# Packed attention with a gated convolution: a subtraction moved to VectorE, one product in plain float32 on small tiles, more store buffers at the end, and a new issue order

## The chip, the cores and the metric

The kernel runs on one core of a Trainium2 chip. The metric is the device time of one execution in microseconds. Five engines work side by side, each through its own queue in order: TensorE (PE in the profile, with PEld for its weight loads), VectorE (DVE), ScalarE (ACT), GpSimd (POOL) and SyncE (SP), whose queue issues all DMAs of this kernel.

## The reference

There are 8 batches, 8 heads, 576 positions and a head size of 64; `p` holds 32 packed queries for each head. Every head attends twice, and the result goes through a gated convolution:

```python
p_packed = sm_attn(p, k, v)                # 32 x 64 for each batch and head
out = sm_attn(q, p_packed, p_packed)       # 576 x 64 for each batch and head
x = out.transpose(0, 2, 1, 3).reshape(B, S, H * D)
gate_pre = sum(conv_w[k] * xp[:, k:k + S, :] for k in range(5))   # xp: 4 rows of zeros ahead of x
gate = 1.0 / (1.0 + np.exp(-gate_pre))
val = x @ w_val
result = (gate * val) @ w_out              # 8 x 576 x 512
```

`sm_attn` is a softmax over scaled scores with 1e-9 added to the sum, and a product with the values. The weights of the gated part come as 64-bit floats and are turned into pairs of 32-bit words on the chip.

## The kernel before, in words

Positions and channels are laid so that 128 partitions are always in use. The eight heads of a batch form two groups g of four heads; a group's 32 packed queries of four heads fill 128 partitions. The 576 positions are two halves of 288.

Each batch goes through these steps; the letter is the stream's name in the order table.

- K, V, Q, P load a batch's inputs (SP), L the weights. C, W and O turn the convolution weights, `w_val` and `w_out` into float32 words (ACT, DVE and POOL in turn).
- k and q: PE turns blocks of k and q (tiles kpt and qpt), ACT copies them to SBUF (kT, qT). k also turns p (pTt, pT).
- a: scores `s<-kT,pT` on PE, their maximum nb on DVE, the exponential a1 on ACT, its turn on PE (at) with a copy (a1t), then the product pv on PE. ACT writes it, divided by the sum, twice side by side into ppd; DVE writes it again times a mask of ones and zeros into pp, so that each head has zeros beside it.
- p: PE turns ppd (ppTt), ACT copies it (ppT).
- s: scores `s<-qT,ppT` for each group; DVE transposes 32x32 blocks (t2), takes the maximum mx; POOL subtracts it, ACT takes the exponential.
- t: DVE sums (sm) and inverts (rs), POOL multiplies, DVE transposes back (a2). ACT rounds a2 to the type float32r (a2h), and DVE writes the rest (a2l).
- w: wp = ppT times the value weights on PE, and again a rounded part wph (ACT) and a rest wpl (DVE).
- x: the attention's output for the convolution. pp too is split (pph on ACT, ppl on POOL), and PE makes three products for each pair of heads: pph with a2h, ppl with a2h, pph with a2l. ACT copies the result into xp behind its zeros, which POOL writes.
- g: the gate, sig: one product on ACT, four multiply-adds on DVE (`sig<-xp,cw,sig`), a tanh on ACT, for each of four blocks n4 of 128 channels.
- v: val = 12 float32r products on PE for each block; DVE multiplies with the gate (`sig<-sig,val`), ACT rounds it (gvh), and POOL writes the rest (gvl). The last of all 32 blocks is on DVE.
- o: the output product, 12 float32r products of gvh, gvl with woh, wol for each of nine chunks of 128 rows of a pair of batches (four in the even batch's turn, five in the odd one's); ACT copies it to osb, and SP stores it. In the last batch the five chunks 4 to 8 are summed block by block in PSUM while the last blocks of val are made; chunks 5 and 7 are copied by DVE.

Tiles named by a tag take turns in a small number of buffers (`NB`). A tile's next use waits until the last reader of its buffer is done. PSUM gives two "big" tiles, shared by s, x, wp and val, three "mid" tiles and one "out" tile. osb has two buffers, a2 one, t2 two.

The order of the work is a table (`ORDER`): each token takes one step (or, with .n, n steps) of one stream for one batch, for example `g3.2`. A step issues one or a few instructions, and each engine runs its own in the order in which the table issues them. Nothing is moved later; a wait on one engine holds everything behind it in that engine's queue. Line 94 of the profile is the helper that issues every instruction, so that groups go by tile names.

Of the kernel before, what the change touches and what calls it, by code (L numbers as in the profile page):

```python
# [48 lines left out]
ORDER = """
K0 L0.3 V0 P0 W0.13 L0 W0 L0 W0 L0 Q0 W0 K0 W0 k0 P1 W0 k0.4 W0 k0.2 W0 C0 W0 k0 C0 a0 W0 C0 W0 a0 W0 a0 q0 C0  # L50
O0 C0 q0.2 C0 O0 q0.2 C0 O0 q0 k0 O0 C0 k0.2 O0 L0 k0.2 V0 O0.2 K1 L0 k0 K1 O0 a0 Q0 O0 L0 k1 P2 a0 k1 O0 a0.3
O0 a0.4 O0 a0.2 O0.2 a0.2 O0 a0.6 O0.2 a0.2 O0 k1 a0.2 O0 p0 x0 k1.2 p0 x0 k1.2 s0 k1 O0.2 w0 s0 O0 x0 s0 a1 w0
O0 k1 s0 a1 k1.2 w0 a1 s0 q0 O0 k1.2 t0 q0.2 k1 q0.2 a1 O0 q0 t0 s0 V1 a1 V1 O0.3 Q1 t0 a1 Q1 a1.2 K2 O0 a1.2 s0
P3 a1.2 k2 t0 s0 k2 O0 a1 O0.2 s0 a1 t0 x0 s0 O0 a1.4 x0.2 t0 a1.2 x0.2 O0 a1.4 g0 t0 a1 p1 a1 q1 p1 g0 q1.2 w1
q1 t0 q1 g0 t0 w1 O0 g0 q1.2 w1 O0 q1.2 s1 O0 k2 q1 O0 s1 q1 K2 k2.2 V2 O0 s1 q1 Q2 k2.2 V2 k2 Q2 s1 K3 a2 P4 O0
s1.2 a2 s1 a2 k2 g0 k2.2 s1 g0 t0 v0 k2 g0 s1 t1 k2 s1 x0 v0 t1 k2 k3 | v0 a2 g0 x0 q2 k3 a2 v0 x0 q2 t1 q2 a2.3
x0 g0 v0 a2 q2 g0 x1 t1 x1 a2 q2 a2 t1 a2 q2.2 g0 a2.2 q2 t1 g0 x1 q2 g0 x1 v0 t1 a2 k3 q2 a2 x1 K3 x1 a2 V3 k3
g0 k3 Q3 v0 q2 P5 t1 k3.2 v0 q2 a2 t1 v0 k3 g0 a2 x1 t1 a2.3 g0 k3 a2.2 k3 g0 k3 a2.2 g0 p2 a3 g0 v0 p2 g0 k3.2
s2 v0 a3 k3 k4 v0 s2 a3 q3 s2 a3 q3 V3 g0 Q3 v0 K4 k4 a3 s2 K4 P6 a3.2 g0 a3 q3 s2 w2 g0 a3 q3 t2 g0 x1 a3 q3
a3.2 w2 v0 t2 a3.2 w2 v0 s2 q3 v0 g1 t2 o0 a3.2 t2 a3 g1 t2 s2 v1 o0 g1 s2 a3 g1 q3 a3.2 s2 x1 q3 o0 a3 Q4 o0 V4  # L60
x1 g1 s2 g1 t2 g1 v1 a3 t2 o0 k4 a3.2 o0 v1 g1 x1 k4 V4 t2 a3 v1 p3 x1 v1 a3 p3 t2 g1 x2 s3 t2 g1 q3 k4 s3 x2
q3.2 k4 o0 g1 q3 Q4 s3 g1 x2 g1 s3 v1.2 g1 q4 s3 k4 v1 q4.2 o0 K5 s3 k4 o0 q4 g1 k4 a4 s3 k4.2 g1 v1 k4 s3 g1 o0
a4 s3 g1.2 v1 a4 g1 s3 g1 v1 x2 o0 q4 g1 x2.2 o0 v1 q4 Q5 q4 x2 v1 q4 g1.2 x2.2 t3 g2 k4 v1 t3 x2 q4 K5 k4 k5 x2
v1 P7 g2 a4 q4 t3 x2 v1 o1 k5 a4 t3 x3 g2 a4.2 x3 t3 a4 o1 k5 t3 a4.2 o1 v2 k5 a4 g2 t3 a4 o1 a4 g2 t3 g2.2 v2
t3 q4 g2 v2 k5 Q5 t3 a4 q4 k5 g2 k5 o1 V5 w3 a4.2 v2 o1 k5 a4 K6 a4 k5 g2 a4.2 w3 o1 g2 k5 w3 a4 x3 g2.3 v2 o1
g2 o1 g2 o1 v2 g2 v2 g2 v2 g2 v2 o1 g2 o1 k5 g2 a4 x3 k5 v2 a4.2 g2 x3.2 v2 g2 V5 k5 a4 x3 a4 p4 v2 a5 K6 k5 p4
v2 g2 a5 x3 g3 a5 g3 o1 v2 g3 v2 g3 a5 v2 o1 v3 o1 a5 g3 a5 o2 a5 g3.2 v3 g3 v3 g3 a5 o2 k6 s4 v3 a5 o2 k6 x3 s4
q5 x3 a5 g3 x3 q5 a5 v3 s4 x3 g3 x4 s4 g3 a5 q5 g3 v3 o2 x4 s4 x4 g3 a5 q5 v3 t4 v3 a5 o2 s4 o2 a5.2 t4 V6 a5.2
q5 s4 a5.2 v3 q5 Q6 g3 a5 t4 g3 q5 t4 a5 s4 k6 q5 a5 w4 g3 k6 t4 g3 q5 k6 s4 g3 v3 a5 k6 w4 g3 x4 V6 o2 v3 g3 s4
w4 v3 x4 a5 q5 a5 t4 p5 o2 k6 g3 p5 q5 o2 k6.2 q5 t4 x4 Q6 k6 K7 s5 x4 g3 k6 s5 v3 g3 x4 t4 g4 k6 s5 t4 a6 g4 k6  # L70
v3 s5 q6 k6 K7 o2 a6 q6 v3 g4 s5 t4 a6 g4 t5 a6 o2 s5 o2 v3 a6 o3 s5 a6 t5 a6 s5 g4 t5 s5 g4 v4 g4 s5 g4 a6 o3
q6 v4 a6.2 o3 t5 x4 g4 a6.2 v4 o3 t5 a6 g4 q6 x4 t5 v4 a6 o3 x4 o3 t5 a6.2 V7 a6 v4 x4 g4 x5 t5 x5 g4 q6 a6 g4
x5 v4 x5 Q7 a6.2 q6 g4 w5 x5 g4 a6 v4 x5 g4 t5 q6 x5 a6 t5 o3 a6 g4 q6 w5 v4 g4 w5 g4 a6 o3 g4 q6 o3 a6.2 k7 g4
p6 q6 V7 v4 k7 g4 p6 g4 q6 v4 g4 x5 k7 Q7 x5 g5 s6 k7 g5 x5 k7 v4 g5 x5 k7 o3 s6 v4 q6 x5 s6 x6 g5 x6 v4 s6 o3.2
g5 s6 k7 v4 w6 g5 k7 t6 v4 s6 g5 o3 v4 s6 w6 s6 t6 w6 s6 k7 t6 o3 v5 k7 g5 o3 s6 g5 t6 o4 v5 g5 v5 t6 g5 k7 o4
t6 x6.2 g5 o4 a7 v5 k7 x6 k7 a7 g5 o4 t6 k7 a7 g5 t6 g5 x6 t6 a7 o4 t6 x6 o4.2 g5 a7 g5 a7.2 g5.2 a7 q7 a7.2 g5
o4 v5 a7 o4 g5 q7 g5 a7 q7 a7 v5 a7 q7 g5 v5 o4 a7.2 v5 g5 a7 g6 x6 g6.2 a7 o4 x6 a7 g6 a7 o4 v5 x6 g6 a7 g6 a7
v5 q7 g6 x6 a7 g6 v5 a7 q7 g6 q7 x6 v5.2 a7.2 q7 x7.2 p7 v5 q7 p7 q7.2 g6 s7 v5 g6 w7 q7 s7 v5 g6 o5 g6 s7 w7 x7
g6 s7 w7 v6 o5 g6 s7 o5 g6 s7 v6 o5 g6 v6 s7 g6 v6 t7 g6 v6 g6 o5 s7 t7 o5.2 v6 s7 t7 v6 g6 s7 t7 v6.2 o5.2 g6
o5 t7.2 v6 t7 v6 x7 g6 o5 x7.2 t7 v6 o5.2 g6 t7 x7.2 t7 g7 x7 g7 o5 v6 g7 o5 x7 g7 x7 v6 x7 g7 v6 g7 v6 o6 g7.2  # L80
v7 o6 g7 o6 g7 o6 v7 g7 v7 g7 v7 g7 v7 o6 g7 o6 g7 o6 v7 g7 v7 g7 v7.2 o6 g7 o6 g7 o6 v7 g7 v7 g7 v7.2 o6.2 g7
o7 g7.2 v7.2 o7 v7 o7.17
"""


# [574 lines left out]
```

## Time and profile before

| | |
|---|---|
| time, median of 3 runs | 331.21 us (329.43 to 331.38) |
| the profiled execution: its own time, its span | 330.79 us, 329.0 us |
| PE busy, weight loads | 287.6 us (87%), 220.6 us |
| DVE busy | 259.0 us (79%) |
| ACT busy | 215.3 us (65%) |
| POOL busy | 123.2 us (37%) |
| DMA | 43.47 MB, 132 GB/s over the span |
| mean granted TensorE clock | 0.976 of full |

The span is the time from the first to the last instruction of the core, and the execution's own time has some 1.8 us around it. A busy PE is not a PE at its peak: matmuls overlap, and a matmul's recorded duration is longer than its place in the queue. Where PE's rate matters, the distance from one group's start to the next group's start is read instead. "x16" behind a row is the number of instructions in it; a plain float32 product of this kernel shows as two records.

### The profile page before, as it was taken

To read this page: it belongs to the slowest core of one execution; us is meant where nothing else is said; L and a number is where in the kernel's file an instruction comes from. 1 tells how busy PE (TensorE), PEld (TensorE's weight loads), DVE (VectorE), ACT (ScalarE), POOL (GpSimd) and SP (SyncE) were. 2 spreads that over 40 slices of the span, in tenths; PEclk is the share of its full clock that TensorE was granted. 3 is DMA by queue.
4 is the path that set the end of the run, shared out by engine and by line. 5 is a ranking of instruction groups with operands and counts; after the bars stand their busy time and mean duration, and the time that the engine had idled before them with its cause. 6 is when DMAs were issued, how large, how long until landed. Compare 5 with 4: busy or idle time off the path is not lost.

```text
span 329.0 us, 7252 instructions
## 1 busy us (share of the span) xinstructions
PE 287.6 (87%) x2932; PEld 220.6 (67%) x2932; DVE 259.0 (79%) x381; ACT 215.3 (65%) x440; POOL 123.2 (37%) x115
## 2 busy tenths in 40 slices
PE   0157987979989999999999898989999999999990
...
DVE  0794288689999999997797999998997899776600
...
PEclk9999997699999999999999999999999999999996
...
GB/s 197 232 255 263 257 162 239 108 230 108 211 217 135 187 166 136 90 241 92 157 34 173 118 237 37 175 87 126 32 66 34 32 35 38 70 53 64 34 24 135
DMA packets 42474, 43.47 MB, mean 132 GB/s; under 512 B 6085, under 2 KB 36805, under 8 KB 42442
## 3 DMA queue, kind: packets, MB, share of 16 engines
...
q8 instruction: 23, 0.38, 0.5%
...
## 4 chain that ended last, share of the span: by engine, by line
PE 40%; DVE 31%; ACT 17%; issue 4%; DMA 3%; POOL 3%; SPq 1%; ACTq 0%; POOLq 0%
DVE sig L94 16%; PE o L94 15%; PE val L94 8%; ACT sig L94 4%; DVE a2l L94 3%; PE x L94 3%; PE s L94 3%; PE kpt L94 3%; PE pv L94 2%; DVE sm L94 2%; PE at L94 2%; DVE t L94 2%; DVE nb L94 2%; DMA wv_words<-in_moe_w_val_dram 2%; PE qpt L94 2%
## 5 line engine op out<-in xcount | busy, mean ns | idle before, releaser
L94 DVE SCALAR_TENSOR_TENSOR sig<-xp,cw,sig 128x576 f32<-128x576 f32 x128 | 122.6, 958 | 11.6 <-ACT sig L94 10.1
L94 POOL TENSOR_TENSOR gvl<-sig,gvh 128x576 fp32r<-128x576 f32 x31 | 49.1, 1584 | 80.0 <-ACT gvh L94 77.0
L94 PE MATMUL o<-woh,gvh 128*128 128x512 f32 x144 | 58.6, 407 | 0.8 <-ACT osb L94 0.8
L94 PE MATMUL o<-woh,gvl 128*128 128x512 f32 x144 | 56.5, 392 | 0.1
L94 PE MATMUL o<-wol,gvh 128*128 128x512 f32 x144 | 56.5, 392 | 0.0
L94 PE MATMUL val<-a2h,wph 128*128 128x288 f32 x128 | 39.6, 309 | 0.5 <-ACT a L94 0.5
L94 PE MATMUL val<-a2l,wph 128*128 128x288 f32 x128 | 37.9, 296 | 0.9 <-DVE a2l L94 0.9
L94 ACT COPY osb<-o 128x512 f32<-128x512 f32 x34 | 19.8, 582 | 28.3 <-PE o L94 22.6
L94 PE MATMUL val<-a2h,wpl 128*128 128x288 f32 x128 | 37.9, 296 | 0.0
L94 PEld LDWEIGHTS o<-woh,gvh 128*128 128x128 f32 x144 | 27.0, 188 | 10.3 <-issue 2.3
L94 ACT CAST gvh<-sig 128x576 fp32r<-128x576 f32 x32 | 21.7, 678 | 17.7 <-DVE sig L94 17.6
L94 POOL TENSOR_TENSOR t<-t,mx 128x576 f32<-128x576 f32 x16 | 24.2, 1513 | 22.0 <-DVE mx L94 22.0
L94 PEld LDWEIGHTS o<-woh,gvl 128*128 128x128 f32 x144 | 27.1, 188 | 6.6 <-POOL gvl L94 0.5
L94 ACT ACTIVATE sig<-sig 128x576 f32<-128x576 f32 x32 | 21.9, 686 | 13.1 <-DVE sig L94 12.9
L94 PEld LDWEIGHTS o<-wol,gvh 128*128 128x128 f32 x144 | 27.1, 188 | 4.6
L94 POOL TENSOR_TENSOR t<-t,rs 128x576 f32<-128x576 f32 x16 | 20.0, 1248 | 23.0 <-DVE rs L94 15.8
L94 DVE SCALAR_TENSOR_TENSOR sig<-sig,val 128x576 f32<-128x576 f32 x32 | 23.7, 741 | 5.6 <-PE val L94 3.0
L94 PE MATMUL qpt<-ident,qm 96*128 96x96 f32 x192 | 26.1, 270 | 1.1 <-ACT kT L94 1.1
L94 PE MATMUL kpt<-ident,km 96*128 96x96 f32 x192 | 26.8, 276 | 0.1
L94 PEld LDWEIGHTS val<-a2h,wph 128*128 128x128 f32 x128 | 24.2, 189 | 3.6 <-ACT a L94 1.2
L94 PEld LDWEIGHTS qpt<-ident,qm 96*128 96x128 f32 x192 | 21.0, 155 | 7.3 <-issue 4.3
L94 PEld LDWEIGHTS kpt<-ident,km 96*128 96x128 f32 x192 | 20.9, 156 | 6.9 <-issue 4.7
...
## 6 DMA issues: line engine op xcount, KB each, us to landing
...
```

Source lines behind the costliest of these rows:

```text
L94: made = getattr(self.engine, op)(*args, **kw)
```

## The change

Five things are changed.

1. gvl, the rest of the gated value, is written by DVE for all 32 blocks.
2. x is made by plain float32 products: for each of four heads one product of ppd (32 partitions, the first of its two copies, 64 columns) with a2 (32 partitions, 288 positions), on tiles of 32 rows and 64 columns of PE's array. Head hl uses rows 32 hl on, columns 64 (hl % 2) on, and writes PSUM bank hl // 2 of the tile. The mask, pp, pph and ppl are gone, ppd has two buffers.
3. So x waits for a2 and ppd alone, and a2's one buffer is held until PE has made x.
4. In the last batch the five chunks 4 to 8 each have a buffer of their own: 4 and 6 keep osb's two, 5 and 7 take t2's two, and 8 takes a2's.
5. The order table is new throughout.

```diff
 NB = {
- 'pp': 2,
- 'ppd': 1,
+ 'ppd': 2,
  'ppT': 2,
- 'pph': 1,
- 'ppl': 1,
...
 ORDER = """
-K0 L0.3 V0 P0 W0.13 L0 W0 L0 W0 L0 Q0 W0 K0 W0 k0 P1 W0 k0.4 W0 k0.2 W0 C0 W0 k0 C0 a0 W0 C0 W0 a0 W0 a0 q0 C0
+x0 L0.5 P0 W0.2 K0 W0 K0 W0 Q0 W0 P1 W0.3 V0 L0 W0 V0 Q0 W0.5 C0 L0 k0 W0 k0 P2 C0 W0 C0 W0 k0 C0 W0 C0 k0.4 K1
...
-    pairs = [slice(2 * NP * pr, 2 * NP * pr + 2 * NP) for pr in range(2)]
-    mask = const.tile([P, 2, D], F32, name="mask")
-    nc.gpsimd.memset(mask, 0.0)
-    for hl in range(4):
-        nc.gpsimd.memset(mask[heads[hl], hl % 2, :], 1.0)
...
-        pp = st["pp", b] = tile_of("pp", [P, G, 2, D], F32, f"pp_{b}")
...
             act.mul(ppd[:, g], pv2, rs)
             yield
-            dve.scalar_tensor_tensor(pp[:, g], pv2, rs, mask, op0=ALU.mult, op1=ALU.mult)
-            yield
...
-        a2 = tile_of("a2", [P, G, S], F32, f"a2_{b}")
+        a2 = st["a2", b] = tile_of("a2", [P, G, S], F32, f"a2_{b}")
...
-        act.copy(pph, pp)
-        yield
-        pool.tensor_tensor(ppl, pp, pph.bitcast(F32), op=ALU.subtract)
-        yield
...
-                ah, al = st["ah", b], st["al", b]
+                pp, a2 = st["ppd", b], st["a2", b]
                 xps = big(f"x_{b}_{g}_{half}")
-                for n, (w, x) in enumerate(((pph, ah), (ppl, ah), (pph, al))):
-                    for pr in range(2):
-                        pe.matmul(
-                            xps[:, pr, :HS],
-                            w[pairs[pr], g, :],
-                            x[pairs[pr], g, hc],
-                            start=(n == 0),
-                            stop=(n == 2),
-                        )
+                for hl in range(4):
+                    pe.matmul(
+                        xps[D * (hl % 2) : D * (hl % 2) + D, hl // 2, :HS],
+                        pp[heads[hl], g, 0, :],
+                        a2[heads[hl], g, hc],
+                        start=True,
+                        stop=True,
+                    )
...
-            (dve if b == B - 1 and n4 == NC - 1 else pool).tensor_tensor(
+            dve.tensor_tensor(
                 lo, gv, hi.bitcast(F32), op=ALU.subtract
             )
...
-            osb = tile_of("osb", [P, DM], F32, f"osb_{b}_{c}")
+            if b == B - 1 and c % 2:
+                osb = tile_of("t2", [P, G, NBLK, NP], F32, f"osb_{b}_{c}")
+                osb = osb.rearrange("a g y z -> a (g y z)")[:, :DM]
+            elif b == B - 1 and c == 8:
+                osb = tile_of("a2", [P, G, S], F32, f"osb_{b}_{c}")[:, 0, :DM]
+            else:
+                osb = tile_of("osb", [P, DM], F32, f"osb_{b}_{c}")
```

On SP's queue the first loads stand in another order. Before (km, vm, qm and p are inputs of batch 0 unless a name comes a second time; wv_words, cw_words and wo_words are the three weights):

```order
L94 DMA km_0_84<-in_k_dram 96x4x384
L94 DMA wv_words<-in_moe_w_val_dram 64x1024 x6
L94 DMA vm_0_95<-in_v_dram 96x4x384
L94 DMA p_97<-in_p_dram 128x2x64 x2
L94 DMA wv_words<-in_moe_w_val_dram 64x1024 x2
L94 DMA cw_words<-in_moe_conv_w_dram 5x1024
L94 DMA wo_words<-in_moe_w_out_dram 128x1024
L94 DMA qm_0_125<-in_q_dram 96x12x128
L94 DMA km_1_128<-in_k_dram 96x4x384
```

And in the changed kernel:

```order
L90 DMA wv_words<-in_moe_w_val_dram 64x1024 x8
L90 DMA cw_words<-in_moe_conv_w_dram 5x1024
L90 DMA p_94<-in_p_dram 128x2x64 x2
L90 DMA km_0_100<-in_k_dram 96x4x384
L90 DMA km_1_103<-in_k_dram 96x4x384
L90 DMA qm_0_106<-in_q_dram 96x12x128
L90 DMA p_109<-in_p_dram 128x2x64 x2
L90 DMA vm_0_116<-in_v_dram 96x4x384
L90 DMA wo_words<-in_moe_w_out_dram 128x1024
```

The value weights now go first as a whole, and batch 0's second k group (km_1) stands ahead of the first block of `w_out` instead of behind it.

On PE, around the first val of batch 0, this stands before in rows 66 to 71 (s_1_1 belongs to batch 1, its second group; kpt_1 to batch 2):

```order
L94 MATMUL s_1_1_793<-qT_1_710,ppT_677 32x288 x8
L94 MATMUL kpt_1_0_809<-ident,km_1_750 128x96 x4
L94 MATMUL kpt_1_1_816<-ident,km_1_750 128x96 x4
L94 MATMUL val_0_824<-a2h_479,wph_439 128x288
L94 MATMUL val_0_824<-a2h_479,wpl_440 128x288
L94 MATMUL val_0_824<-a2l_480,wph_439 128x288
```

In the changed kernel it stands in rows 45 to 50, with x of batch 0 ahead of it and its three products replaced by four on smaller tiles:

```order
L90 MATMUL qpt_0_2_584<-ident,qm_0_276 128x96 x4
L90 MATMUL at_0_2_590<-ident,a_1_0_496 96x128 x2
L90 MATMUL x_1_0_597<-a_0_425,ppd_263 64x288 x4
L90 MATMUL pv_0_604<-vm_0_311,a1t_0_565 32x64 x24
L90 MATMUL x_1_1_632<-a_0_425,ppd_263 64x288 x4
L90 MATMUL val_0_643<-a2h_426,wph_407 128x288
```

Ahead of the first val stood 68 rows, and 49 stand there now: five groups of kpt, three of qpt, three of s, three of at, one each of pv, ppTt and wp have moved behind it, and two more groups of x have come ahead of it.

On DVE, a piece of batch 0's gates in the changed kernel (gvl is the moved subtraction, sig_0 to sig_2 are blocks of batch 0, t_1 and a_1 belong to batch 1):

```order
L90 SCALAR_TENSOR_TENSOR sig_2_857<-xp_1_557,cw,sig_2_857 128x576
L90 TENSOR_REDUCE nb_2_1_892<-s_2_1_866 128x1
L90 TENSOR_TENSOR gvl<-sig_0_545,gvh 128x576
L90 TENSOR_SCALAR sm_2_0_830<-sm_2_0_830 128x1
L90 RECIPROCAL sm_2_0_830<-sm_2_0_830 128x1
L90 SCALAR_TENSOR_TENSOR sig_2_857<-xp_1_557,cw,sig_2_857 128x576
L90 TENSOR_REDUCE sm_1_937<-t_1_751 128x18
```

Before, the same instruction stood on POOL, between its other work:

```order
L94 TENSOR_TENSOR t_1_724<-t_1_724,rs_1_842 128x576
L94 TENSOR_TENSOR gvl<-sig_1_838,gvh 128x576
L94 TENSOR_TENSOR gvl<-sig_2_1004,gvh 128x576
L94 TENSOR_TENSOR t_2_1162<-t_2_1162,mx_2_1163 128x576
L94 MEMSET xp_1_1271 128x4x2
```

Between the first `sig<-sig,val` of batch 0 and that of batch 1 DVE had 54 instructions before; it has 61 now: four gvl, two more `sig<-xp`, one more each of t, mx, nb and wpl, three word conversions, and three pp and one a2l fewer, besides small ones.

More of the change, by code (lines that the diff above doesn't have):

```diff
@@ L49 @@
 ORDER = """
-K0 L0.3 V0 P0 W0.13 L0 W0 L0 W0 L0 Q0 W0 K0 W0 k0 P1 W0 k0.4 W0 k0.2 W0 C0 W0 k0 C0 a0 W0 C0 W0 a0 W0 a0 q0 C0
[L51 to L79, printed above, removed]
@@ L80 @@
-o5 t7.2 v6 t7 v6 x7 g6 o5 x7.2 t7 v6 o5.2 g6 t7 x7.2 t7 g7 x7 g7 o5 v6 g7 o5 x7 g7 x7 v6 x7 g7 v6 g7 v6 o6 g7.2
-v7 o6 g7 o6 g7 o6 v7 g7 v7 g7 v7 g7 v7 o6 g7 o6 g7 o6 v7 g7 v7 g7 v7.2 o6 g7 o6 g7 o6 v7 g7 v7 g7 v7.2 o6.2 g7
-o7 g7.2 v7.2 o7 v7 o7.17
+x0 L0.5 P0 W0.2 K0 W0 K0 W0 Q0 W0 P1 W0.3 V0 L0 W0 V0 Q0 W0.5 C0 L0 k0 W0 k0 P2 C0 W0 C0 W0 k0 C0 W0 C0 k0.4 K1
+W0 C0 L0 k0.2 W0 k0.2 C0 W0 a0 k0 C0 W0 k0 a0 k0 K1 q0 W0 a0.2 W0 k1 q0.2 a0 k1 P3 q0.2 a0.3 L0 a0.2 Q1 a0 q0
+a0.3 O0 V1 a0.7 O0 a0 O0 a0 O0.2 a0 p0 V1 O0.2 p0 O0 s0 O0 q0 w0 s0 q0 O0 s0 q0 O0 w0 s0 O0 w0 s0 q0.2 Q1 O0 t0
@@ new lines @@
+k1 q0 s0 k1 O0 k1 t0 s0 k1.2 K2 O0 k1 a1 t0 O0.2 s0 t0 x0 a1 O0 s0 k1 t0 a1 O0 k1.2 s0 k1.2 K2 t0 x0.2 k1 k2 P4
+O0 x0 a1 O0 t0 g0 a1 q1 O0 g0 x0 a1.3 k2 g0 q1.2 a1.2 t0 q1.2 a1.2 g0 Q2 t0 x0 a1 O0 a1 q1 g0 x0.2 O0 a1 V2 g0
+t0 v0 x0 O0 a1 g0 O0.2 a1 g0 q1 a1.2 O0 v0 a1.2 O0 a1 q1 g0 a1 O0.3 k2 O0 a1 p1 V2 k2.2 p1 q1 k2.2 q1 s1 g0 k2
+K3 k2 O0 a2 k2 s1 k2 O0 q1 k2 a2 k2 O0.2 Q2 w1 s1 K3 q1 O0 g0 q2 s1 a2 g0 w1 O0 s1.3 w1 k2 k3 P5 O0 g0 q2.2 s1
+a2 q2 x1 g0 q2 s1 | v0 a2 k3 Q3 q2 k3 v0 a2 v0 k3 s1 a2 g0 k3 a2 t1 q2 k3 a2.2 q2.2 a2 g0 a2 t1 q2 k3 v0 a2.2 k3
@@ new lines @@
+K4 g0 v0 k3 q2 a2 V3 k3.2 t1 Q3 g0 a2.2 g0 x1 v0 t1 g0 v0 q2 x1 t1 a2 t1 k3 x1 a2 k3 g0 t1 a2.2 x1 K4 v0 a2.2 k3
+g0 v0 k4 V3 a2 a3 P6 p2 t1 p2 a3 t1 s2 v0 a3 q3 g0 q3 v0 s2 g0 x1 t1 g1 x1 v0 g1 v0 a3 x1 s2 k4 x1 g1 s2 a3 q3
+k4 x1 g1 a3 q3.2 Q4 a3 w2 g1 s2 q3 v0 o0 g1 t2 g1 w2 g1 t2 k4 w2 v1 o0 g1 o0 t2 o0 g1 t2 v1 g1 v1 t2 s2 g1 x2.2
+v1 g1 o0 g1 q3 a3 k4 x2 o0 s2 o0 a3 q3 g1 k4 s2 g1 s2 v1 g1 o0.2 s2 o0 v1 g1.2 t2 v1 g1 t2 a3 v1 o0 v1 a3 o0 x2
+g1 a3 k4 t2 a3.2 k4 K5 v1 x2 q3 g1 a3 k4 V4 v1 a3.3 g1 k4 q3 v1.2 x2 g1 a3 q3 g2 v1 k4 a3 Q4 x2 q3 g2 v1 a3 g2
@@ new lines @@
+a3.2 x2 v1 x2 k4 V4 a3 g2 k4 t2 o1 K5 k4 t2 x2 g2.3 v2 o1 g2 o1 g2 a4 v2 p3 o1 p3 a4 v2 g2 a4 v2 g2 s3 o1 x3 w3
+g2 o1 s3 g2 q4 s3 v2 w3 g2 s3 q4 w3 q4 o1 q4 v2 s3 g2 v2 t3 s3 o1 g2 t3 a4 o1 s3 q4 k5 o1 a4 q4 Q5 k5 g2 P7 a4.2
+g2 s3 g2 t3 s3 a4 o1 k5 g2 x3 a4 o1 s3 a4 o1 t3 v2 a4 g2 x3 k5 t3 g2 v2 t3 o1.2 g2 t3 x3 v2 g2 a4 k5 a4.2 v2 t3
+k5.2 v2 a4 v2 V5 k5 K6 a4 t3 x3.2 t3 a4 k5 g3 v2 x3 a4 k5 g3 k5 v2 a4 q4 g3 a4 q4 v2 o2 k5 x3 g3.2 a4 g3 x3 a4
+g3 a4 x3 g3 q4 v3 V5 a4 q4 g3 o2 g3 o2.2 v3 g3 v3.2 g3 x4 g3 p4 q4 o2 g3 k5 p4 Q5 a5 k5 g3 o2 s4 q4 K6 o2 a5 s4
```

17 lines of the change are left out of this document (14 added, 3 removed).

## The prediction

> **What bounds the kernel now.** I read the page's busy shares and slices first.
>
> ```profile
> span 329.0 us, 7252 instructions
> PE 287.6 (87%) x2932; PEld 220.6 (67%) x2932; DVE 259.0 (79%) x381; ACT 215.3 (65%) x440; POOL 123.2 (37%) x115
> PE   0157987979989999999999898989999999999990
> DVE  0794288689999999997797999998997899776600
> PEclk9999997699999999999999999999999999999996
> ```
>
> PE has nines from about the tenth slice to the last but one, DVE nearly as many. To price the parts I cut the span where PE starts (15.5), where val of batch 0 and of batch 1 start (69.6, 101.6) and where DVE is done (311).
>
> ```profile
> core 0: us, PE busy (x) PEld busy (x) DVE busy (x) ACT busy (x) POOL busy (x), PEclk, DMA share, GB/s
> 0.00:15.50 15.50, 0.40 (x2) 0.43 (x3) 5.63 (x9) 3.30 (x4) 2.95 (x14) 1.00 0.92 214
> 15.50:69.60 54.10, 43.72 (x534) 28.58 (x532) 36.55 (x65) 38.81 (x88) 26.33 (x23) 0.91 0.96 215
> 69.60:101.60 32.00, 29.44 (x412) 22.07 (x413) 30.14 (x53) 27.67 (x62) 13.52 (x12) 1.00 0.84 177
> 101.60:311.00 209.40, 204.26 (x1945) 161.80 (x1944) 185.29 (x256) 143.81 (x284) 80.42 (x67) 1.00 0.38 103
> 311.00:329.00 18.00, 9.74 (x43) 7.72 (x42) 1.38 (x2) 1.76 (x3) 0.00 (x0) 0.84 0.23 73
> ```
>
> So there are four regimes. Up to 69.6 no engine is full: chains of loads, ACT and DVE set the pace. From 69.6 to 101.6 DVE is at 94%. From 101.6 on PE is at 98% and DVE at 88%: PE sets the end, DVE is close. After PE's last product only stores are left. The marks come from these rows (one product of batch 0's and 1's val, DVE's first use of each, PE's last product):
>
> ```profile
> L94 PE MATMUL val<-a2h,wph x20: 289/294/405, 69.6 to 102.8; 128*128 128x288 f32 x20
> 101.61 0.30 PE L94 MATMUL val<-a2h,wph 128*128 128x288 f32 x1
> 72.78 0.76 DVE L94 SCALAR_TENSOR_TENSOR sig<-sig,val 128x576 f32<-128x576 f32 x1
> 107.35 0.70 DVE L94 SCALAR_TENSOR_TENSOR sig<-sig,val 128x576 f32<-128x576 f32 x1
> 320.35 0.39 PE L94 MATMUL o<-woh,gvl 128*128 128x512 f32 x1
> ```
>
> I sum along PE: start of batch 1's val (101.6), from there to the last product (320.7, so 219.1), and the tail (329.0, so 8.3).
>
> **gvl on DVE.** The groups by shape give the prices, and one row a gate step undisturbed:
>
> ```profile
> L94 DVE SCALAR_TENSOR_TENSOR sig<-xp,cw,sig 128x576 f32<-128x576 f32 x128 | 122.6, 958 | 11.6 <-ACT sig L94 10.1
> L94 DVE TENSOR_TENSOR a2l<-a,a2h 128x576 fp32r<-128x576 f32 x16 | 16.9, 1055 | 1.5 <-ACT a2h L94 1.4
> L94 POOL TENSOR_TENSOR gvl<-sig,gvh 128x576 fp32r<-128x576 f32 x31 | 49.1, 1584 | 80.0 <-ACT gvh L94 77.0 <-PE x L94 2.7 <-POOL t L94 0.3
> L94 POOL TENSOR_TENSOR t<-t,mx 128x576 f32<-128x576 f32 x16 | 24.2, 1513 | 22.0 <-DVE mx L94 22.0
> L94 POOL TENSOR_TENSOR t<-t,rs 128x576 f32<-128x576 f32 x16 | 20.0, 1248 | 23.0 <-DVE rs L94 15.8 <-ACT qT L94 3.2 <-ACT a1t L94 2.6
> L94 POOL TENSOR_TENSOR ppl<-pp,pph 128x256 fp32r<-128x256 f32 x8 | 7.1, 894 | 5.5 <-ACT pph L94 4.6 <-POOL gvl L94 0.9
> L94 DVE TENSOR_TENSOR gvl<-sig,gvh 128x576 fp32r<-128x576 f32 x1 | 0.8, 759 | 0.7 <-ACT gvh L94 0.7
> L94 DVE SCALAR_TENSOR_TENSOR pp<-pv,sm,mask 128x128 f32<-128x128 f32 x16 | 5.4, 338 | 7.3 <-ACT ppd L94 7.2
> 120.99 0.80 DVE L94 SCALAR_TENSOR_TENSOR sig<-xp,cw,sig 128x576 f32<-128x576 f32 x1
> 123.22 4.42 DVE L94 SCALAR_TENSOR_TENSOR sig<-xp,cw,sig 128x576 f32<-128x576 f32 x4
> 125.11 1.91 POOL L94 TENSOR_TENSOR gvl<-sig,gvh 128x576 fp32r<-128x576 f32 x1 [2.30 <-ACT gvh L94]
> ```
>
> DVE gains 31 x 0.759 = 23.5 us and loses the pp writes, 5.4. But POOL slows it: four gate steps that met a gvl on POOL took 4.42 us, not 4 x 0.80 = 3.2. Over all, sig lies 128 x 0.158 = 20.2 above 0.80 and a2l 16 x 0.30 = 4.7 above 0.759: 25 us, for 100.4 us of POOL's two-input work. gvl and ppl are 56.2 of that, so 14 us of slowing go; on the 11 that stay, 31 more such instructions on DVE add 11 x 31 / 144 = 2.4. DVE: 259.0 + 23.5 - 5.4 - 14 + 2.4 = 265.5. Bounds are 23.5 - 5.4 = +18 with no relief and 18 - 25 = -7 with all slowing gone; I take +6.5, since the relief is a share of a measured total. The Trainium skill (SBUF — State Buffer, Who interferes with whom) has it harder: a VectorE instruction with two SBUF inputs and a GpSimd instruction that reads SBUF lock each other out for the whole instruction. By that rule four steps and a 1.91 us gvl would take 5.1 us one after the other, a loss of 1.9 for the row's 1.2, and the relief would be 14 x 1.9 / 1.2 = 22 us, with DVE at 257 or so. The row's 4.42 disagrees, so I keep 14.
>
> In 101.6 to 311 DVE has 209.4 - 185.3 = 24.1 idle us. The net of some +6 fits, so I cost it at nothing there; if that idle time can't be used, it is rival 2. DVE is in order: behind a gvl that waits for ACT's gvh stand gate steps and transposes, and PE's o waits for it. POOL had idled 80.0 us ahead of its gvl, so PE was not held by POOL's rate.
>
> **x in float32.** Groups of x and of s, plain float32 with tiles too, from their start to the next group's start:
>
> ```profile
> 152.58 0.40 PE L94 MATMUL x<-a2h,pph 64*128 64x288 f32 x2
> 152.95 0.29 PE L94 MATMUL x<-a2l,pph 64*128 64x288 f32 x2
> 153.17 0.88 PE L94 MATMUL pv<-vm,a1t 96*32 96x64 f32 x48
> 155.27 0.72 PE L94 MATMUL s<-kT,pT 64*32 64x288 f32 x16
> 155.92 0.40 PE L94 MATMUL val<-a2h,wph 128*128 128x288 f32 x1
> ```
>
> An x group held PE 0.59 us, an s group 0.65. s has eight products over the same 288 columns, the new x four; nothing shows tiles of 32 rows. If the four run side by side as the eight do, x takes at most 0.65: +0.06 x 32 = +1.9. At half of s it would be 0.33, -8; in two turns about 1.1, +16. I take +1.9, the row it is nearest to. ACT's pph, POOL's ppl and the waits for a2h and a2l ahead of x go; what is late next is a2 itself. a2's buffer now waits for PE's x before DVE may transpose the next batch: in the table at least 31 steps lie between, so I cost it at nothing (2 us if PE falls that far behind). ppd has two buffers for the same reason.
>
> **The head.** km_1 was issued late, the second scores waited for it, and with them the chain to the first val:
>
> ```profile
> 14.38 0.60 SPq L94 DMA_DIRECT2D km<-in_k_dram  x1
> 29.32 1.22 PE L94 MATMUL s<-kT,pT 64*32 64x288 f32 x16 [0.82 <-ACT kT L94]
> L94 PE MATMUL s<-qT,ppT x32: 402/556/687, 40.4 to 48.5; 64*32 64x288 f32 x32
> 7.68 1.28 ACT L94 ACT_TABLE_LOAD   x1 [7.68 <-DMA wv_words<-in_moe_w_val_dram]
> 60.67 0.68 ACT L94 CAST a2h<-a 128x576 fp32r<-128x576 f32 x1
> ```
>
> Now km_1 stands fifth on SP, some 4 to 5 us earlier, with vm, qm and wo behind it; I move the q scores from 40.4 to about 35, and with the same 20.3 us from there to the second a2h (60.67) that comes at 55. By ACT's queue: 72 rows stood ahead of that a2h, 60 do now; at (60.67 - 7.7) / 72 = 0.74 each it comes at 52. So val of batch 0 starts at about 55, not 69.6. The 19 rows fewer ahead of it on PE (some 6.5 us of groups) have to be done after it.
>
> From there DVE sets the pace. Between its first uses of the two vals it took 107.35 - 72.78 = 34.6 us for 54 instructions, 0.64 each; 61 now give 39.0, and the added ones are longer (0.76, 0.80) than the pp (0.34) that go: 40.5. DVE then comes to batch 1's at 55 + 3.2 + 40.5 = 98.7, not 107.35. PE, with the 6.5 us, could start that val at 55 + 32.0 + 6.5 = 93.5, but DVE frees its PSUM tiles. I take 97, between the two: 4.6 us gained, of bounds 0 and 8.
>
> **The tail.**
>
> ```profile
> 321.72 0.58 ACT L94 COPY osb<-o 128x512 f32<-128x512 f32 x1 [3.07 <-DMA out_dram<-osb]
> 324.83 0.59 ACT L94 COPY osb<-o 128x512 f32<-128x512 f32 x1 [2.53 <-DMA out_dram<-osb]
> 322.72 2.02 DMA out_dram<-osb
> ```
>
> Copies waited for earlier stores to free osb, and the last ended 325.4, 3.6 ahead of the span's end. With five buffers it follows PE's last product (320.7) and ends at 321.4. What is late next are seven store issues close together on SP: the earlier six start before that copy ends, so I allow 0.3 us of their queue at the end (0 to 2), and the span ends at 321.4 + 0.3 + 3.6 = 325.3. So the tail is 4.6 for 8.3.
>
> **The sum.** 97 + (219.1 + 1.9) + 4.6 = 322.6 for a span of 329.0. The profiled execution took 330.79, 1.8 more than its span; the median of the runs is 331.21, 0.4 more again. So 322.6 + 1.8 + 0.4 = 324.8. About 1% (3.3 us) is what a measurement of this kernel can tell from no change.
>
> **The rivals.**
>
> 1. The head's gain is given back: the new chain meets ACT at once, and batch 1 starts where it did. For it: ACT has 38.8 busy us of 54.1 there and DVE 94% behind it. Then 101.6 + 221.0 + 4.6 + 2.2 = 329.4. Chance 0.22.
> 2. DVE becomes the bound, slower: in 101.6 to 311 it gets 27 gvl, 20.5 us, with collisions only moved to the t steps. If half of the 24.1 idle us can be filled, 8.5 stay: 329.4 + 8.5 = 337.9. It decides from the point where less than 15 of the 20.5 find a place. Against it: 88% there, and the slowing does go with POOL's work. Chance 0.11.
> 3. x runs in two turns. Heads 0 and 1 use different rows of the array but write one PSUM bank, in different partitions; in the rows of s each half of the rows has a bank of its own. The second turn would cost some 0.5 us for each of 28 groups that PE has after the head: 324.8 + 14 = 338.8. No row shows the case; that their partitions differ speaks against it. Chance 0.15. The Trainium skill (TensorEngine Tiling (Array Packing), Gotcha 1: PSUM Pressure) states the rule behind this: different row tiles can't access one PSUM bank at the same time.
>
> **How the numbers follow.** The forecast has 0.52: 324.8, from 318.5 (x at half of s for part of it, head at 93.5) to 328. Faster by over 1% (below 327.9) is the forecast and a quarter of rival 1: 0.57. Within 1%: the rest of rival 1 and the mild ends of 2 and 3: 0.23. Slower (above 334.5): 0.20. The range that leaves out 0.2 goes from 318.5 into rival 2 and 3's lower ends, 336.
>
> **What would show it.** In the profile after: val of batch 0 near 55 and of batch 1 near 97 (69 and over 101 is rival 1); an x group's slot at or below 0.65 (1.1 is rival 3); sig's mean near 0.87, DVE near 265 us with PE still at 97% from batch 1 on (DVE at 97% and PE with waits for gvl or sig: rival 2); the last copy within 1 us of the last product. A clock row that drops again after the head would add time that I don't count.

## The result, and the profile after

The changed kernel takes 319.65 us (median) against 330.44 us for the kernel before on the same chip: a ratio of 0.966, 95% interval 0.9604 to 0.9715, so 10.8 us less. The prediction had 324.8 us, in a range of 318.5 to 336. The profiled execution took 319.36 us, its span is 317.6. Now and then a run is slow, some per cent longer than the others of its kernel (326.35 us here, with 318.24 to 319.95 for the other three): four of the medians in this document, that of the change among them, hold one such run and lie 0.3 to 0.6 us above the median of the fast runs, while ratios and their intervals are of fast runs alone.

The page's busy shares and slices of the changed kernel:

```profile
span 317.6 us, 7342 instructions
PE 284.6 (90%) x2996; PEld 209.2 (66%) x2996; DVE 255.0 (80%) x396; ACT 212.7 (67%) x432; POOL 67.8 (21%) x71
PE   0088786879989999999999999999999999999993
DVE  0983388679999997999789986897998977878771
PEclk9999758899999999999999999999999999999999
```

PE has nines from the thirteenth slice to the last but one, without a break. The span is cut, as in the prediction, at PE's start and at val of batch 0 and of batch 1, and then at the end of PE's last product; the columns are those of the prediction's table:

```profile
14.00:57.65 43.65, 34.59 (x403) 19.92 (x403) 29.48 (x53) 29.55 (x67) 16.46 (x15) 0.84 1.14 238
57.65:98.33 40.68, 36.07 (x510) 24.76 (x507) 35.68 (x58) 36.10 (x80) 15.52 (x14) 1.00 1.00 201
98.33:312.37 214.04, 213.96 (x2089) 164.51 (x2087) 183.75 (x277) 143.15 (x282) 32.93 (x35) 1.00 0.38 99
312.37:317.60 5.23, 0.00 (x0) 0.00 (x0) 0.05 (x1) 0.58 (x1) 0.00 (x0) 0.91 0.62 213
```

And the kernel before, from its val of batch 1 to its last product:

```profile
101.61:320.74 219.13, 213.99 (x1987) 169.52 (x1985) 185.97 (x256) 144.39 (x285) 80.42 (x67) 1.00 0.37 99
```

I call these stages the head (up to batch 1's val), the middle and the tail. The head is 3.3 us shorter (98.33 for 101.61), the middle 5.1 (214.04 for 219.13), the tail 3.0 (5.23 for 8.3). The middle's two rows say where its 5.1 come from: PE is busy for the same 214.0 us in both, though 102 more of its records fall into the middle now, and its idle time went from 5.14 us to 0.08.

The page also follows the chain of work that ended last back from the last instruction, and gives each engine's share of it. Before, and in the changed kernel:

```profile
PE 40%; DVE 31%; ACT 17%; issue 4%; DMA 3%; POOL 3%; SPq 1%; ACTq 0%; POOLq 0%
PE 81%; ACT 8%; DMA 5%; DVE 3%; SPq 1%; issue 1%; ACTq 0%; DVEq 0%
```

In the middle alone, the same view gives the gate steps on DVE (sig) 22.0% of the chain before, as much as o on PE (21.9%). In the change the middle's chain runs over PE but for 0.3%. The chain is one path where others may be nearly as long, so it is a sign and not a proof: PE's busy share of 98% before did not mean that PE alone set the end.

The groups that were to change, by shape (busy us, mean ns of one, idle time of the engine ahead of them):

```profile
L90 DVE SCALAR_TENSOR_TENSOR sig<-xp,cw,sig 128x576 f32<-128x576 f32 x128 | 106.4, 832 | 10.8 <-ACT sig L90 9.4
L90 DVE TENSOR_TENSOR a2l<-a,a2h 128x576 fp32r<-128x576 f32 x16 | 13.7, 855 | 2.4 <-ACT a2h L90 2.2
L90 DVE TENSOR_TENSOR gvl<-sig,gvh 128x576 fp32r<-128x576 f32 x32 | 25.2, 788 | 2.6 <-ACT gvh L90 2.4
```

A gate step (sig) takes 832 ns for 958, and DVE is busy for 255.0 us in all, less than the 259.0 before, with 24 us of gvl added. The chain that ended last, at one place in the middle (start, time, what), shows an x group beside an s group:

```profile
102.86 0.65 PE s L90 x16
103.51 0.65 PE x L90 x8
104.15 0.48 PE qpt L90 x4
```

The end, on ACT:

```profile
309.64 0.59 ACT L90 COPY osb<-o 128x512 f32<-128x512 f32 x1 [1.38 <-PE o L90]
311.03 0.59 ACT L90 COPY osb<-o 128x512 f32<-128x512 f32 x1 [0.81 <-PE o L90]
312.40 0.58 ACT L90 COPY osb<-o 128x512 f32<-128x512 f32 x1 [0.78 <-PE o L90]
```

And the seven store issues on SP's queue:

```profile
310.25 3.94 SPq L90 DMA_DIRECT2D out_dram<-osb  x7
```

No copy waits for a store any more; the last one ends at 312.98, 0.6 behind the last product.

### The profile page after: what moved, and what is told of

It reads as the page before. It is cut to its first block, busy times and chain, and to the rows that moved or that the text cites. A ratio compares the mean times of both kernels' runs of the same rounds, so it can differ in the third digit from the quotient of the medians.

```text
span 317.6 us, 7342 instructions
## 1 busy us (share of the span) xinstructions
PE 284.6 (90%) x2996; PEld 209.2 (66%) x2996; DVE 255.0 (80%) x396; ACT 212.7 (67%) x432; POOL 67.8 (21%) x71
## 4 chain that ended last, share of the span: by engine, by line
PE 81%; ACT 8%; DMA 5%; DVE 3%; SPq 1%; issue 1%; ACTq 0%; DVEq 0%
PE o L90 32%; PE val L90 16%; PE x L90 6%; PE s L90 6%; PE kpt L90 5%; PE qpt L90 5%; PE pv L90 3%; DMA km<-in_k_dram 3%; PE at L90 3%; PE wp L90 3%; DMA wv_words<-in_moe_w_val_dram 2%; DVE sig L90 1%; ACT a1t L90 1%; ACT a L90 1%; ACT wo_top L90 1%; SPq L90 1%
## 5 line engine op out<-in xcount | busy, mean ns | idle before, releaser
L90 DVE SCALAR_TENSOR_TENSOR sig<-xp,cw,sig 128x576 f32<-128x576 f32 x128 | 106.4, 832 | 10.8 <-ACT sig L90 9.4
L90 POOL TENSOR_TENSOR t<-t,mx 128x576 f32<-128x576 f32 x16 | 23.1, 1442 | 47.8 <-DVE mx L90 46.6
L90 POOL TENSOR_TENSOR t<-t,rs 128x576 f32<-128x576 f32 x16 | 22.0, 1372 | 50.1 <-DVE rs L90 44.6
L90 ACT COPY kT<-kpt 128x384 f32<-128x384 f32 x48 | 23.3, 485 | 10.2 <-PE kpt L90 10.0
L90 PEld LDWEIGHTS qpt<-ident,qm 96*128 96x128 f32 x192 | 19.6, 147 | 13.2 <-issue 7.5
L90 ACT COPY qT<-qpt 128x384 f32<-128x384 f32 x48 | 22.9, 485 | 6.9 <-PE qpt L90 6.9
L90 DVE TENSOR_TENSOR gvl<-sig,gvh 128x576 fp32r<-128x576 f32 x32 | 25.2, 788 | 2.6 <-ACT gvh L90 2.4
```

The lines of the kernel that those rows point to most:

```text
L90: made = getattr(self.engine, op)(*args, **kw)
```

## The experiments

In what follows the old order is the table of the kernel before, and the new order that of the changed kernel. The question was what took the 5 us of PE's idle time out of the middle, for which the prediction had 1.9 us the other way. Three theories: A, the operations (gvl off POOL, x with fewer waits) took it; B, the new issue order took it; C, order and operations only work together. So each new operation was put alone into the old order, and taken alone out of the new one.

| kernel | median, us | ratio to before, 95% | batch 1's val | middle | PE idle in it | tail |
|---|---|---|---|---|---|---|
| before | 330.4 to 331.0 | 1 | 101.6 | 219.13 | 5.14 | 8.3 |
| old order, gvl on DVE | 329.37 | 0.993 to 0.998 | 102.7 | 216.33 | 3.51 | 8.3 |
| old order, new x | 329.07 | 0.994 to 0.998 | 100.5 | 219.62 | 3.20 | 8.1 |
| old order, five store buffers | 328.83 | 0.992 to 0.996 | 102.3 | 219.12 | 5.13 | 5.7 |
| old order, all three | 326.47 | 0.984 to 0.991 | 100.6 | 217.69 | 1.98 | 5.7 |
| new order, all three (the change) | 319.65 | 0.960 to 0.972 | 98.3 | 214.04 | 0.08 | 5.2 |
| new order, two store buffers | 321.84 | 0.966 to 0.976 | 98.8 | 214.01 | 0.10 | 7.8 |
| new order, gvl on POOL | 325.80 | 0.981 to 0.994 | 97.8 | 220.69 | 4.94 | 5.2 |
| new order, old x | 339.50 | 1.021 to 1.029 | 107.9 | 223.86 | 7.80 | 5.5 |
| new order, none of the three | 349.81 | 1.053 to 1.063 | 105.4 | 233.87 | 12.26 | 7.7 |

The medians are of timed runs on several chips (the kernel before took 330.4 to 331.0 us on each), the other columns of one profile each; the middle is cut at the first product of batch 1's val and the end of PE's last product, and the idle time is its length less PE's busy time in it.

**The new order with the old operations.** All edits but the order table go back. So that the old x fits in, pph gets a second buffer and mx two for three, pph and ppl are written at the end of the p steps, and in a few places a2's rounding is issued a step earlier, ahead of x.

```diff
-            dve.tensor_tensor(
+            (dve if b == B - 1 and n4 == NC - 1 else pool).tensor_tensor(
                 lo, gv, hi.bitcast(F32), op=ALU.subtract
...
+                for n, (w, x) in enumerate(((pph, ah), (ppl, ah), (pph, al))):
...
+            osb = tile_of("osb", [P, DM], F32, f"osb_{b}_{c}")
```

> The changed kernel's order with all the old operations: gvl on POOL, x from pph, ppl, a2h, a2l, two store buffers at the end (pph gets a second buffer, and a2's rounding is issued a step earlier in a few places, so that the old products can stand where the new ones stand). The whole change took 331 to 319.7, of it 3.3 in the head (batch 1's val at 98.3 for 101.6), 5.1 from there to PE's last product (214.0 for 219.1) and 3.1 in the tail. Theory A (the 5.1 us between come from the operations: PE and DVE no longer wait for POOL's gvl and its slowing): the order alone gives the head's 3 and no more, 327 to 329, with sig near 950 ns. Theory B (the 5.1 us come from the order): head and middle both, 322 to 324, even with POOL doing gvl. Theory C (order and operations need each other): slower than the kernel before, over 333, since a table laid out for gvl on DVE makes PE wait for POOL's 1.58 us each.

Measured: 349.81 us, 5.8% slower than before. B falls in one run: with the old operations the order costs 19 us. That is C's time, but not by the wait that C named. The longest waits of its PE in the middle (us in total, times, longest) are x's:

```profile
PE x L94 <- DVE a2l L94: 5.5, 7, 1.6
PE x L94 <- ACT a2h L94: 3.7, 4, 1.2
PE o L94 <- POOL gvl L94: 1.5, 2, 0.8
```

A part of the 19 us may be the clock, which is lower in this kernel's runs (0.931 to 0.953, before 0.965 to 0.990).

**The old order with all new operations.** a2 gets a second buffer, mx has two for three, and ten steps of batch 3's packed attention stand behind batch 1's last x, since ppd's second buffer would otherwise be written too early.

> The kernel before in its own order with all the new operations: gvl on DVE, x from a2 and ppd in plain float32, five store buffers (a2 gets a second buffer, and ten steps of batch 3's packed attention stand after batch 1's last x, since ppd's second buffer would otherwise be written too early). Theory A: middle and tail move as in the whole change, 5 + 3 us, and the head stays: 322 to 324, DVE near 255 us, sig near 830 ns. Theory B: the tail's 3 us alone, 327 to 329, though DVE's collisions with POOL are gone. Theory C: not below 330.

Measured: 326.47 us, 4.5 less than before, between what A and B expected; the single edits, below, give 1.6 + 1.5 + 1.8 = 4.9, so they about add up. A is right for 4.5 of the 10.8 us, and the rest needs order and operations together (C). In the middle the operations took 1.4 of the 5.1:

```profile
100.61:318.30 217.69, 215.71 (x2039) 163.87 (x2037) 187.35 (x277) 144.51 (x281) 33.37 (x34) 1.00 0.38 100
```

PE's idle time fell from 5.14 to 1.98, but PE is busy for 215.71 us instead of 213.99. Part of that is x, part a thing of its own (the placement runs, below).

**gvl alone, out of the new order and into the old one.**

```diff
-            (dve if b == B - 1 and n4 == NC - 1 else pool).tensor_tensor(
+            dve.tensor_tensor(
                 lo, gv, hi.bitcast(F32), op=ALU.subtract
```

> The changed kernel with gvl back on POOL (the last of 32 on DVE as before), all else as changed. Theory A, with gvl as what brings the middle's 5 us: 324 to 326, sig back near 920 ns for 832 and DVE within 3 us of 255, since the 24 us less of gvl are nearly paid by the slowing. Theory B: 319 to 321. Theory C: over 328, with PE's o waiting for POOL.

> The kernel before with gvl on DVE and nothing else. Theory A: 325 to 327, sig near 850 ns. Theory B: 330 to 332, no change outside a few tenths of a per cent. The rival of the prediction in which DVE becomes the bound would show here as well: 335 or more, DVE at 95% from batch 1 on with PE waiting for sig or gvl.

Measured: 325.80 without it in the new order (6.2 slower than the change) and 329.37 with it in the old one (1.6 faster than before). The second is less than A expected and more than B. The new order with gvl on POOL, from its page and its groups:

```profile
PE 286.3 (88%) x2996; PEld 208.9 (65%) x2996; DVE 254.8 (79%) x365; ACT 212.5 (66%) x432; POOL 115.8 (36%) x102
...
L90 DVE SCALAR_TENSOR_TENSOR sig<-xp,cw,sig 128x576 f32<-128x576 f32 x128 | 125.9, 984 | 17.1 <-ACT sig L90 15.6
L90 POOL TENSOR_TENSOR gvl<-sig,gvh 128x576 fp32r<-128x576 f32 x31 | 48.4, 1562 | 72.1 <-ACT gvh L90 72.1
```

And the old order with gvl on DVE:

```profile
PE 285.6 (87%) x2932; PEld 220.5 (67%) x2932; DVE 263.5 (81%) x412; ACT 215.8 (66%) x440; POOL 75.5 (23%) x84
...
L94 DVE SCALAR_TENSOR_TENSOR sig<-xp,cw,sig 128x576 f32<-128x576 f32 x128 | 109.2, 853 | 7.8 <-ACT sig L94 6.4
```

In the new order gvl on DVE costs DVE nothing: 254.8 us busy with gvl on POOL, 255.0 with it on DVE. sig gives back 125.9 - 106.4 = 19.5 us and a2l another 0.8 of the 24.4 that 31 more gvl take; most of the rest is in no group, since records on DVE overlap in part and its busy time counts that once. In the old order sig gives back 122.6 - 109.2 = 13.4, a2l 1.4, and DVE is 4.5 us busier (263.5). The middles of the two, the new order's with gvl on POOL first:

```profile
97.78:318.47 220.69, 215.75 (x2089) 164.17 (x2087) 185.52 (x250) 143.74 (x283) 74.36 (x62) 1.00 0.36 96
```

```profile
102.65:318.98 216.33, 212.82 (x1987) 169.52 (x1985) 189.15 (x284) 144.83 (x285) 37.93 (x40) 1.00 0.37 101
```

With gvl on DVE the middle is shorter in both orders, by 6.6 and by 2.8 us: so it does follow gvl. PE's idle time is 4.9 and 1.6 of that; the rest is busy time of the same number of products, so a busy PE hides some waiting. Two causes are possible, the shorter way from gvh to o and the faster gate steps. No run parts them, but the new order's chain speaks for the gate steps: with gvl on POOL they have 18.5% of the middle's chain, and no gvl on POOL is in it. The rival in which DVE becomes the bound shows in neither.

**x alone.** In the old order the new x (with a2's second buffer, mx's two and the ten moved steps), in the new order the old one (with all that the old x needed above).

```diff
-                ah, al = st["ah", b], st["al", b]
+                pp, a2 = st["ppd", b], st["a2", b]
...
-                for n, (w, x) in enumerate(((pph, ah), (ppl, ah), (pph, al))):
+                for hl in range(4):
```

> The kernel before, in its own order, with the new x alone (a2 gets a second buffer, and ten steps of batch 3's packed attention stand behind batch 1's last x). From the run with all new operations less the ones with one each, x is worth: middle 217.7 against 216.3 with gvl on DVE alone, so 1 to 2 us longer between batch 1's val and the last product (0.05 us more for each of 28 groups, as forecast), and the head 1 to 2 us shorter: 329.5 to 331.5 in all. Rival: x's fewer waits and the 12 us less of pp and ppl work on DVE and POOL shorten the middle too: 327 to 329, sig near 910 ns for 958. The rival of the prediction in which row tiles take turns: 338 or more, an x slot of 1.1 us for 0.59.

> The changed kernel with the old x: pp written by DVE, pph and ppl, three products of rounded parts (a second pph buffer, a2's rounding issued a step earlier in a few places so that it stands ahead of x). The order with all the old operations took 349.8 us, with only gvl on POOL 325.8. If x's operands are what that order can't do without (theory C for x: PE, standing behind a2 without room for a2h and a2l, waits for them), this is 335 to 342, with x waiting some 10 us for a2h and a2l and batch 1's val near 105. If it was the two together (POOL doing gvl and ppl, DVE slowed), this is near the sum of small parts: 322 to 326.

Measured: 329.07 in the old order, 1.5 less than before, the head 1.1 shorter and the middle 0.5 longer. That is between what was expected and the first rival: PE's idle time in the middle fell from 5.14 to 3.20 us, but its busy time rose by 2.4, and sig took 937 ns for 958. In the new order, as expected, 339.50, 19.9 more than the change. What the old x does there, from the waits of its middle (us in total, times, longest):

```profile
PE x L94 <- ACT a2h L94: 3.7, 4, 1.2
PE x L94 <- DVE a2l L94: 3.7, 6, 1.6
```

The new table issues x right behind a2. The old x needs a2h and a2l first, and PE stands for 7.4 us in the middle alone. Of the head's 9.6 us a part may be the lower granted clock of that run there (0.85 from 59 to 108 us, 1.00 in the change), so I don't count it.

**The store buffers alone.**

```diff
-            if b == B - 1 and c % 2:
-                osb = tile_of("t2", [P, G, NBLK, NP], F32, f"osb_{b}_{c}")
...
+            osb = tile_of("osb", [P, DM], F32, f"osb_{b}_{c}")
```

> The changed kernel with only the two store buffers of osb at the end. The prediction's step on the tail: the last two copies wait again 2.5 to 3 us each for stores, the last copy ends 5 us behind the last product for 0.6, and the kernel is 2.5 to 3.5 us slower than the changed one: 322 to 323.5, batch 1's val and PE's last product where they were within 1 us. Rival: the new order already spreads the chunks, so that two buffers do: 319 to 320.5.

> The kernel before with five store buffers at the end and nothing else: 327.5 to 328.5 for 331, last copy within 1 us of the last product, span's end 5.2 to 5.7 behind it for 8.3. Rival: stores share the DMA queue, the last store takes as much longer: 330 to 331.

Measured: 321.84, so some 2 us more than the change, and 328.83, 1.8 less than before, each a little less than expected. The interval of the first meets that of the change, so it rests on the tails (7.8 and 5.2 us) more than on the times. ACT's last two copies in the new order with two buffers:

```profile
313.81 0.59 ACT L90 COPY osb<-o 128x512 f32<-128x512 f32 x1 [3.09 <-DMA out_dram<-osb]
316.93 0.59 ACT L90 COPY osb<-o 128x512 f32<-128x512 f32 x1 [2.54 <-DMA out_dram<-osb]
```

The step stands in both orders: the copies wait for stores, and with five buffers they don't. The middle stays within 0.03 us in both pairs.

**A longer output product.** In four of the kernels so far an o group of twelve products took 2.91 us from its start to the next group's, at the median, in the six others 2.85 to 2.86. In the compiled program of the four gvh and gvl begin on a multiple of 64 bytes in their partitions, and woh and wol 32 bytes past one. In the others all four begin 32 past. (The profiles hold no addresses; they show what moving the tiles does.) The four also share mx's two buffers for three, which may be what moved the tiles. So 32 unused bytes were put ahead of gvh, or ahead of nearly all tiles.

```diff
+    late.tile([P, 8], F32, name="shift")
     gvh = late.tile([P, NC, 2 * S], F32R, name="gvh")
```

> The old order with all new operations, and 32 unused bytes of each partition ahead of gvh, so that gvh and gvl begin 32 bytes past a multiple of 64, as in the kernels before and after, instead of on one. In the run without these bytes an o product group took 2.906 us from its start to the next group's, in before and after 2.85 to 2.86; the four kernels in which gvh begins on a multiple of 64 all have the longer one, the six others the shorter. Theory (placement): the group takes 2.86 again, 36 groups make 1.7 us, and the time is 324.3 to 325.2 for 326.5. Rival (the longer groups come from something else that these four kernels share, as a2's or sig's place): 326 to 327, 2.906 us.

> The changed kernel with 32 unused bytes ahead of gvh and nothing else, so that gvh and gvl begin on a multiple of 64 and w_out's parts woh and wol 32 past one. Theory (placement): o groups of 2.90 us for 2.86, 1.5 to 2 us slower than the changed kernel, 321 to 322. Rival: no difference, 319 to 320.

> The changed kernel with 32 unused bytes ahead of nearly all tiles, so that gvh, gvl, woh, wol, the value weights and the rounded a2 all begin on a multiple of 64. If the long o group comes from gvh standing otherwise than woh in the 64 bytes (theory M), this is as the changed kernel, 319 to 320, o groups of 2.86. If it comes from gvh or gvl on a multiple of 64 as such (theory N), 321 to 322, o groups of 2.90.

Measured: 325.29 (0.981 to 0.987), 320.99 (0.968 to 0.974) and 319.72 (0.963 to 0.970). The times alone don't separate these from the kernels without the bytes (326.47, 319.65), since the intervals meet. The middles do; the change with gvh moved, its middle and its group of o with gvl:

```profile
100.52:315.57 215.05, 214.94 (x2089) 164.40 (x2087) 183.76 (x277) 143.08 (x282) 32.94 (x35) 1.00 0.38 98
```

```profile
L90 PE MATMUL o<-woh,gvl 128*128 128x512 f32 x144 | 57.0, 396 | 0.0
```

With nearly all tiles moved, the same two rows:

```profile
99.12:313.18 214.06, 213.97 (x2089) 164.38 (x2087) 183.72 (x277) 143.12 (x282) 32.95 (x35) 1.00 0.38 99
```

```profile
L90 PE MATMUL o<-woh,gvl 128*128 128x512 f32 x144 | 56.5, 392 | 0.0
```

Moving gvh alone costs 1.0 us of busy PE; moving woh with it takes it back. That speaks for theory M: it is how they stand to each other, not gvh's place as such. Four profiles of the new order (the change, all tiles moved, two store buffers, and k earlier, below) have middles of 214.01 to 214.06 us, so 1.0 is far outside their spread. In the old order the bytes won only 0.66 of the 1.7 us that were expected (PE busy 215.05 for 215.71; o groups 2.89, not 2.86), so something else in that layout lengthens o too, and stays open. The old-order runs with the new x, and the new-order runs with the old one, carry about 1 us of this that is not x's.

**An earlier start of the keys.** The head still has much idle PE, so one run tried for more.

```diff
-x0 L0.5 P0 W0.2 K0 W0 K0 W0 Q0 W0 P1 W0.3 V0
+x0 L0.2 P0 K0 L0 K0 L0.2 W0.2 W0 W0 Q0 W0 P1 W0.3 V0
```

> The changed kernel with batch 0's p and both its k groups ahead of some of the eight loads of the value weights: p and the first k group behind four, the second behind six, none of the other loads moved past another. In the changed kernel PE does nothing before p lands at 14.1 and then waits 2.4 us for k. If the head hangs on k, PE starts 1.5 to 3 us earlier and batch 1's val too: 317 to 318.5. If it hangs on ACT, which has the weights' conversions and then the scores' chain in its queue, the weights come later by what p and k come earlier, and nothing is gained: 319 to 320.5.

Measured: 321.91 us (0.971 to 0.978), some 2 more than the change, a loss that neither expectation had, and batch 1's val at 102.5. ACT in its head:

```profile
13.76 0.66 ACT L90 ACTIVATE wv_top<-wv_words 128x512 f32<-128x512 f32 x1 [4.96 <-DMA wv_words<-in_moe_w_val_dram]
19.24 0.65 ACT L90 ACTIVATE cw_top<-cw_words 5x512 f32<-5x512 f32 x1 [4.81 <-DMA cw_words<-in_moe_conv_w_dram]
19.80 0.36 ACT L90 ACTIVATE pT<-pTt 128x256 f32<-128x256 f32 x1
```

And the longest waits of its PE up to 98 us (in total, times, longest):

```profile
PE pTt L90 <- DMA p<-in_p_dram: 8.9, 1, 8.9
PE kpt L90 <- ACT pT L90: 7.3, 1, 7.3
```

PE did start 5 us earlier, at 8.9, and then waited 7.3 us for pT: that copy stands on ACT behind conversions of weights, and these waited for loads that now came later (4.96 and 4.81 us). So this head hangs on ACT's queue. It suggests that the weights' early place in the change is part of its gain, which no run shows by itself.

## Why the prediction was right, and where not

The direction holds, the result lies in the range, and none of the three rivals came as a whole. That it lies in the range is luck in part: the lower end of 318.5 was to cover a faster x and an earlier head. Neither came, and what came instead was in no bound. By the prediction's own steps:

- **The middle, the mis-sized term.** "219.1 + 1.9 = 221.0"; measured 214.04. The step carried PE's time from batch 1's val to the last product over as it was, and added x. But 5.1 us of that was PE's idle time, which stands in the prediction's own table (204.26 busy of 209.40 us), and the text costed what the change does to it at nothing: gvl since POOL was idle for 80 us, x's waits since a2 "is late next", the order not at all. Behind that stood "PE sets the end", read from the busy share of 98%; the page's chain, 31% of it on DVE, said otherwise before the change. POOL's rate was indeed no bound. By the runs the three operations take 3.2 us of idle time (5.14 to 1.98), the order with them the last 1.9. x's +0.05 us a group is there (0.645 for 0.595) but was nearly covered: the middle grew by 0.5 with the new x alone, which includes the longer o groups.
- **DVE.** Forecast 265.5, measured 255.0. The mechanism holds (sig is 16.2 and a2l 3.2 us less than before, 19.4 for a forecast net of 11.6), but the price of a collision was read wrongly. Of the four gate steps of 4.42 us only the last lost time. Around POOL's gvl, recorded from 125.11 to 127.02, the last two on DVE are:

```profile
124.92 0.82 DVE L94 SCALAR_TENSOR_TENSOR sig<-xp,cw,sig 128x576 f32<-128x576 f32 x1
125.77 1.86 DVE L94 SCALAR_TENSOR_TENSOR sig<-xp,cw,sig 128x576 f32<-128x576 f32 x1
```

The first ends at 125.74, gvl 1.28 us behind it, and the second 0.61 behind gvl; the gvl at 116.84 and at 140.10 show the same distances to 0.01 us. So the two took turns, and both records include the wait for the other. With 1.28 us for gvl instead of the recorded 1.91, four steps of 0.80 one after the other with it take 4.48, near the row's 4.42. The row agrees with the rule of the Trainium skill (SBUF — State Buffer, Who interferes with whom), by which the two engines lock each other out for the whole instruction; the prediction held the row against it. Its estimate by that rule, DVE at 257, came nearer to the 255.0, but it too took the 1.91 for gvl's own time. How much is lost depends on what meets: gvl's move alone takes 14.8 us off sig and a2l in the old order, 20.3 in the new one.
- **The head.** Forecast 55 and 97, measured 57.65 and 98.33; in three other profiles of the new order with all three operations, placement apart, or with two store buffers, batch 0's val came at 55.1 to 56.0 and batch 1's at 98.8, 99.1 and 100.5. So the gain is 1 to 3 us, not 4.6. DVE's way between its first uses of the two vals took 41.9 us, forecast 40.5. Between the vals themselves PE, DVE and ACT are each busy for some 36 of the 40.68 us; which of them holds that stage was not tested. Nor was the granted clock, which from PE's start to batch 0's val was 0.84 in the change and 0.96 with two store buffers.
- **The tail.** Forecast 4.6, measured 5.2. The waits went as said; the 0.3 us for seven store issues close together was too small. They end at 310.25 + 3.94 = 314.19, 1.2 us behind the last copy, and in the old order the tail is 5.7.
- **Rival 2, DVE as the bound.** It did not come. Its time of 337.9 stands on rival 1's 329.4; by itself, on the forecast's 324.8, it would have been 333.3.
- **Rival 3, x in two turns.** An x group takes 0.645 us, as long as an s group of twice as many products, not 1.1. The rule of the Trainium skill (TensorEngine Tiling (Array Packing), Gotcha 1: PSUM Pressure), that different row tiles can't access one PSUM bank at the same time, cost nothing that these rows show, though the four products share two banks.
- **The sum.** Head 1.3 us later than forecast, middle 7.0 shorter, tail 0.6 longer: 5.0 us, the difference of the two spans (322.6 and 317.6).
